# Fused attention and expert routing on one core: the first v kept on the chip, a new product order in the value step, and other places for loads and pads

## The chip, the core and the metric

The kernel runs on one core of one Trainium2 chip. The metric is the device time in microseconds of that core from the first to the last instruction of an execution, as the median of several runs. Five engines work side by side, each with its own stream of instructions in a fixed order: PE (TensorE, matrix products; PEld are its weight loads), DVE (VectorE), ACT (ScalarE), POOL (GpSimd) and SP (SyncE, which here issues most DMA transfers; its rows are named SPq).

## The reference, cut to what matters

```python
# u, v: (8, 2496, 256)   z: (8, 2496, 64)
scores = (z @ z^T) / S                      # per batch, S = 2496
attn   = maximum(scores, 0) ** 2
x      = u * (attn @ v)                     # 8 * 2496 = 19968 rows of 256
xn, en = x / (norm(x) + 1e-6), expert_emb / (norm(expert_emb) + 1e-6)
logits = xn @ en.T / tau                    # 8 experts
e      = argmax(logits);  gate = softmax(logits)[e]
out    = gate * (maximum(x @ w1[e], 0) @ w2[e])   # w1: 256 x 1024, w2: 1024 x 256
```

## The kernel before

Everything is computed with pairs of 16-bit numbers: a float32 operand is scaled by a power of two and split into a high and a low half, and a product becomes two or three products of halves. The scale comes from the largest absolute value, so z and v of a batch have to be scanned (`scan_load`, `scan_max`, `scale_pieces`) before they can be split (`z_split`, `v_split`).

**First part: attention and routing.** Each of the 8 batches has 20 key tiles `s` of 128 rows (the last has 64) and 5 query groups `g` of 512 columns (the last has 448): 800 steps. A step computes, where the score tile isn't had by symmetry, two products for the scores (`scores`), then ACT's Relu and Square make the probabilities, and DVE splits them into a high part (a cast) and a low part (a subtraction) in `parts`. `values` then adds to the two accumulators of the group: for each half `k` of the 256 output columns, high v times high part (`va`, `ph`), high v times low part (`va`, `pl`), low v times high part (`vb`, `ph`). A tile with `s // 4 > g` is also turned by a DMA transpose on SP into `tt`, for use in a later group. The split parts lie in five buffers (`hl`); scores run three tiles ahead (LOOK), parts two. When a group is finished, `route` makes a queue of some 20 small pieces, of which one is done per step of the next group: multiply by u, turn, norms, logits, choice of the expert, place, and at the end four indirect writes (`scatter`, POOL) of the group's rows into `xs` in DRAM, sorted by expert. In between the next batch is scanned, loaded and split (`ahead`), and the 8 experts' weights are scaled, split and written to DRAM (`weights`, 80 pieces, one in 8 steps, buffers wr1, wr2 and wo).

Ahead of all that stands the start: z of batch 0 is scanned and split, v is scanned in 8 pieces through 2 buffers, and then loaded a second time tile by tile for the split. The small constants for the routing (identity, triangle, normalised expert embeddings) are made in the same place.

**Second part: experts.** The sorted rows are worked off in slots: 61 slots of 256 rows (phase A, whose rows come from the first seven batches), 10 of 256 (C) and 17 of 128 (B), with 4 spare ones. `slot_x` loads a slot's rows from `xs` with a DMA transpose, `slot_w` loads the expert's weights into one of 4 buffers (after the first ones under a condition: only if the expert changed), `slot_up` and `slot_down` are the two layers. The rows of slot k + 3 are asked for in slot k. The last pieces of routing, the tables of the phases C and B and the `pads` (8 rows of zeros behind each expert's rows) are popped from the same queue between the products of the first slots. Rows and weights go through SP, one instruction after the other. POOL writes the results to the output by an indirect DMA.

PE's order is that of the code (`manual_schedule`), SP's too from `slot_first` on. The other engines, and SP before that, follow a scheduler.

Of the kernel before, what the change touches and what calls it, by code (L numbers as in the profile page):

```python
# [19 lines left out]
P = 128  # L20
# [24 lines left out]
def relu2_attention_then_moe(ctx, tc, zT, uT, v, emb, tau, w1, w2, ident, tri, iota_e, out):  # L45
    nc = tc.nc
    B, DQ, S = zT.shape
    D = uT.shape[1]
# [14 lines left out]
    twin = S % P == DQ  # L63
# [11 lines left out]
    xs = dram.tile([E * CAP + TB, ROW], F32, name="xs")  # L75
    wsd = dram.tile([E, P, WR1 + WR2], F16, name="wsd")
# [18 lines left out]
    SCAN = S * DQ // (P * ZSCANS)  # L95
    assert S * DQ == ZSCANS * SCAN * P and DQ % ZSCANS == 0 and S % VSCANS == 0
    scan = {}

    def scan_load(b, what, i):

        t = wk.tile([P, SCAN], F32, name="scan", tag="scan", bufs=2)
        if what == "z":
            src = zT[b, i * (DQ // ZSCANS):(i + 1) * (DQ // ZSCANS), :]
        else:
            src = v[b, i * (S // VSCANS):(i + 1) * (S // VSCANS), :]
        nc.sync.dma_start(t, src.rearrange("a c -> (a c)").rearrange("(p w) -> p w", p=P))
# [60 lines left out]
    def z_load(b, c0):  # L167
        zt = zpool.tile([P, ZC], F32, name="zt", tag="zt", bufs=3)
        c1 = min(c0 + ZC, SP)
        m = min(c1, S) - c0  # L170
        if c1 > S and not twin:
            nc.gpsimd.memset(zt, 0.0)
        for h in (0, DQ):
            if m > 0:
                nc.sync.dma_start(zt[h:h + DQ, :m], zT[b, :, c0:c0 + m])
            if c1 > S and twin:
                nc.sync.dma_start(zt[h:h + DQ, m:m + DQ], zT[b, :, S - DQ:])
# [17 lines left out]
    def v_load(b, s):  # L195
        n = min(P, S - s * P)
        vt = wk.tile([P, D], F32, name="vt", tag="vt", bufs=VAHEAD + 2)
        if n < P and not twin:
            nc.gpsimd.memset(vt, 0.0)
        nc.sync.dma_start(vt[:n], v[b, s * P:s * P + n, :])  # L200
        if n < P and twin:
            nc.sync.dma_start(vt[n:], v[b, s * P:s * P + n, :])
        vraw[b, s] = vt

    def v_split(b, s):
# [3 lines left out]
        if twin and s == NST - 1:  # L209
# [53 lines left out]
    def values(acc, b, g, s, ph, pl, ks=(0, 1)):  # L263
# [3 lines left out]
        for k in ks:  # L267
            va = vv[:, k * P:(k + 1) * P]
            vb = vv[:, D + k * P:D + (k + 1) * P]
            if twin and last:  # L270
                nc.tensor.matmul(acc[k][:, :n], va, ph[:, :n], start=first, stop=False)
                nc.tensor.matmul(acc[k][:, :n], vb, pl[:, :n], start=False, stop=True)
                continue
            nc.tensor.matmul(acc[k][:, :n], va, ph[:, :n], start=first, stop=False)  # L274
# [11 lines left out]
    def route(b, g, acc, ut):  # L286
# [131 lines left out]
        def scatter(j):  # L418
            def f():
                m = min(P, n - j * P)  # L420
                nc.gpsimd.indirect_dma_start(  # L421
                    xs[:, :], bass.IndirectOffsetOnAxis(ap=loc["dsti"][:m, j:j + 1], axis=0),
                    row[:m, j, :], None)
            return f
# [99 lines left out]
    nc.vector.memset(ones_f, 1.0)  # L524
    for what, i in SCANS[:ZSCANS]:
        scan_load(0, what, i)
    nc.sync.dma_start(idt, ident)
    z_tiles(0)
    ZN = ceil_div(SP, ZC)
    for k in range(min(3, ZN)):  # L530
        z_load(0, k * ZC)
    for what, i in SCANS[:ZSCANS]:
        scan_max(0, what, i)
    for f in scale_pieces(0, "z"):
        f()
    for k in range(min(2, ZN)):
        z_split(0, k * ZC)
    for what, i in SCANS[ZSCANS:]:
        scan_load(0, what, i)
        scan_max(0, what, i)  # L540
    for q in range(min(VAHEAD, NST)):
        v_load(0, q)
# [4 lines left out]
    for i in range(min(LOOK - 1, len(direct))):  # L547
        halves[direct[i]] = parts(*direct[i], probs.pop(direct[i]))
    zk = 2
# [530 lines left out]
```

## Time and profile before

| | us |
|---|---|
| median of 3 runs (lowest to highest) | 2231.42 (2230.69 to 2233.59) |
| the profiled execution's own time | 2233.2 |
| its span, first to last instruction | 2231.4 |
| PE busy | 2149.6 (96%) |
| PE weight loads busy | 1411.3 (63%) |
| DVE busy | 1412.9 (63%) |
| ACT busy | 1089.9 (49%) |
| POOL busy | 349.7 (16%) |

The page gives the busy time of each engine over the span and in 40 slices, with the clock granted to PE and the share of the 16 DMA engines. The ends of PE's products are modelled, so a busy PE isn't a PE at its peak; what counts there is how far apart two products start. Attention runs to about 1352 us, phase A begins there. A row of the order of time has the start, the duration, the engine, the line, the operation, what it writes and reads with the shapes, and in brackets how long the engine was idle before it and what released it.

### The profile page before, as it was taken

What the parts mean: (1) busy time and instruction counts of PE and PEld (TensorE: products, weight loads), DVE (VectorE), ACT (ScalarE), POOL (GpSimd) and SP (SyncE); (2) the same over time, 40 slices, a digit from 0 to 9 for tenths busy, and PEclk for the clock granted to TensorE, in tenths of its full rate; (3) what the DMA queues carried; (4) which work ended last, traced back from release to release, by engine and by line L of the source; (5) the groups of instructions that cost most, each with busy time, mean ns of one, the idle gap of its engine ahead of it and who ended that gap; (6) DMA issues with size and microseconds to landing.
All of it is one profiled execution on the core that took longest, in us unless ns stands there. A gap on an engine that the chain in (4) does not pass through costs nothing. (4 is left out here: it accounts for less than half of the span.)

```text
span 2231.4 us, 42157 instructions
## 1 busy us (share of the span) xinstructions
PE 2149.6 (96%) x14634; PEld 1411.3 (63%) x14634; DVE 1412.9 (63%) x4174; ACT 1089.9 (49%) x2193; POOL 349.7 (16%) x428
## 2 busy tenths in 40 slices
PE   5999999999999999999999998999999999999997
PEld 2445445445445444445445556888888888888986
DVE  7788889788789888889788754433333333333332
ACT  5667667667568567667667542222222222222211
POOL 0011111111111111111111111211111111111211
PEclk9999999999999999999999999999999999999999
DMA  7948866765947857766756435433323332257383
GB/s 196 208 110 216 172 172 144 185 155 140 229 103 180 203 114 196 167 175 144 171 122 126 97 82 154 130 70 89 87 56 87 95 87 49 56 143 202 103 211 91
DMA packets 525322, 307.74 MB, mean 138 GB/s; under 512 B 444069, under 2 KB 486446, under 8 KB 516912
## 3 DMA queue, kind: packets, MB, share of 16 engines
q1 hardware_dynamic: 509920, 263.76, 51.2%
q0 software_dynamic: 15184, 41.24, 5.4%
q8 instruction: 117, 1.92, 0.4%
q14 instruction: 101, 0.83, 0.1%
HBM read 279.49 MB, written 59.60 MB: 152 GB/s over the span
## 5 line engine op out<-in xcount | busy, mean ns | idle before, releaser
L237 ACT ACTIVATE a<-sc 128x512 f32<-128x512 f32 (+1 forms) x480 | 283.1, 590 | 181.7 <-PE sc L235 126.8
L238 ACT ACTIVATE a<-a 128x512 f32<-128x512 f32 (+1 forms) x480 | 300.0, 625 | 13.5
L276 PEld LDWEIGHTS <-vv 128*128 128x128 f16 x1520 | 149.0, 98 | 183.7 <-issue 15.6
L876 POOL DMA_INDIRECT out_dram<-ot,me x159 | 155.0, 975 | 669.7 <-DVE ot L875 365.3
L871 PE MATMUL po<-w,hl 128*128 128x256 f16 x928 | 253.0, 273 | 0.0
L870 PE MATMUL po<-w,hh 128*128 128x256 f16 x928 | 252.9, 273 | 0.0
L869 PE MATMUL po<-w,hh 128*128 128x256 f16 x928 | 252.9, 273 | 0.0
L275 PEld LDWEIGHTS <-vv 128*128 128x128 f16 x1520 | 148.9, 98 | 160.9 <-issue 5.0
L421 POOL DMA_INDIRECT xs<-row,dsti x160 | 175.3, 1096 | 480.5 <-DMA xs<-row,dsti 344.1
L274 PEld LDWEIGHTS <-vv 128*128 128x128 f16 x1520 | 148.9, 98 | 157.9 <-issue 1.3
L274 PE MATMUL acc<-tt,vv 128*128 128x512 f16 (+1 forms) x640 | 236.4, 369 | 0.0
L275 PE MATMUL acc<-tt,vv 128*128 128x512 f16 (+1 forms) x640 | 236.3, 369 | 0.0
L276 PE MATMUL acc<-tt,vv 128*128 128x512 f16 (+1 forms) x640 | 236.2, 369 | 0.0
L875 DVE TENSOR_SCALAR ot<-po,me,w 128x256 f32<-128x256 f32 x116 | 58.3, 540 | 219.8 <-PE po L871 218.5
L234 PE MATMUL sc<-z 128*128 128x512 f16 (+1 forms) x480 | 182.4, 380 | 4.6 <-DVE z L191 4.6
L235 PE MATMUL sc<-z,z 128*128 128x512 f16 (+1 forms) x480 | 182.5, 380 | 0.0
L870 PEld LDWEIGHTS <-hh 128*128 128x128 f16 x1272 | 124.8, 98 | 20.4 <-issue 5.8
L871 PEld LDWEIGHTS <-hl 128*128 128x128 f16 x1272 | 124.8, 98 | 14.8
L869 PEld LDWEIGHTS <-hh 128*128 128x128 f16 x1272 | 124.8, 98 | 14.5
L323 ACT COPY x<-pt 128x264 f32<-128x264 f32 x160 | 59.6, 372 | 95.7 <-PE pt L313 85.6
L869 PE MATMUL po<-wb,hh 128*128 128x256 f16 x344 | 94.7, 275 | 5.5 <-DMA wb<-wsd 5.5
L870 PE MATMUL po<-wb,hh 128*128 128x256 f16 x344 | 94.8, 275 | 0.0
(4179 smaller groups left out, 5146.3 us busy)
## 6 DMA issues: line engine op xcount, KB each, us to landing
w<-wsd SPq DMA_DIRECT2D x64, 1026.0 KB
wa<-wsd SPq DMA_DIRECT2D x46, 1024.0 KB
w<-wsd SPq DMA_DIRECT2D x42, 1024.0 KB
wb<-wsd SPq DMA_DIRECT2D x24, 1026.0 KB
scan<-in_v_dram SPq DMA_DIRECT2D x64, 312.0 KB
vt<-in_v_dram SPq DMA_DIRECT2D x152, 128.0 KB
ut<-in_uT_dram SPq DMA_DIRECT2D x32, 512.0 KB
wr<-in_w_dram SPq DMA_DIRECT2D x16, 1024.0 KB
```

The lines of the kernel that those rows point to most:

```text
L234: nc.tensor.matmul(sc[:, :n], z1[:, ss], z1[:, t0:t0 + n], start=True, stop=False)
L235: nc.tensor.matmul(sc[:, :n], z1[:, ss], z2[:, t0:t0 + n], start=False, stop=True)
L237: state["at"] = nc.scalar.activation(a[:, :n], sc[:, :n], AF.Relu, scale=2.0 ** -SHIFT).ins
L238: nc.scalar.activation(a[:, :n], a[:, :n], AF.Square)
L274: nc.tensor.matmul(acc[k][:, :n], va, ph[:, :n], start=first, stop=False)
L275: nc.tensor.matmul(acc[k][:, :n], va, pl[:, :n], start=False, stop=False)
L276: nc.tensor.matmul(acc[k][:, :n], vb, ph[:, :n], start=False, stop=last)
L421: nc.gpsimd.indirect_dma_start(xs[:, :], bass.IndirectOffsetOnAxis(ap=loc["dsti"][:m, j:j + 1], axis=0), row[:m, j, :], None)
L869: nc.tensor.matmul(o, hh[:, f, t], wh, start=(f == 0), stop=False)
L870: nc.tensor.matmul(o, hh[:, f, t], wl, start=False, stop=False)
L871: nc.tensor.matmul(o, hl[:, f, t], wh, start=False, stop=(f == NF - 1))
L876: nc.gpsimd.indirect_dma_start(out, bass.IndirectOffsetOnAxis(ap=me.bitcast(U32)[:, j, 1:2], axis=0), ot[:, j, :], None, bounds_check=N - ...
```

## The change

1. z is put into DRAM twice on top of itself (128 rows), and z and v are padded with copies of their last 64 rows, so that a z chunk and a v tile are one load each. Scans are 640 columns wide instead of 624.
2. v of batch 0 is loaded once, in five pieces of four tiles, into buffers that later hold expert weights (`v_first`). The scan reads these pieces (1,024 columns each), and so does the split.
3. At the start four score tiles are computed ahead of v's scale instead of three; ACT and DVE follow the written order there. One z scan and the identity are issued from ACT. The routing constants are made at steps 6 and 14 of group 0, and the experts' weights begin at step 26 instead of 20.
4. `values` does all products with the high part first, for both halves, and then those with the low part.
5. The x loads of phase A name the last scatter of batch 6 as what they wait for, and none of batch 7's.
6. The second-layer load for the second buffer moves behind the x load of slot 3, `pads` 12 places down the queue (two slots), a slot's expert number and flag are read once, and the writes to the output don't wait for each other.

```diff
     def scan_max(b, what, i):
         if i == 0:
-            scan[b, what] = sml.tile([P, ZSCANS if what == "z" else VSCANS], F32, name="smx" + what)
+            n = ZSCANS if what == "z" else VSCANS if b else NV0
+            scan[b, what] = sml.tile([P, n], F32, name="smx" + what)
...
     def z_load(b, c0):
...
-        for h in (0, DQ):
-            if m > 0:
-                nc.sync.dma_start(zt[h:h + DQ, :m], zT[b, :, c0:c0 + m])
...
+        nc.sync.dma_start(zt[:, :c1 - c0], zT[b, :, c0:c1])
...
+    def v_first(i):
+        if not v0:
+            v0.extend([wp.tile([P, W1], F32, name="v0a", tag="wr1"), wp.tile([P, W2], F32, name="v0b", tag="wr2"),
+                       wp.tile([P, 2 * max(W1, W2)], F16, name="v0c", tag="wo").bitcast(F32)])
...
+        nc.sync.dma_start(t, v[0, q * P:(q + n) * P, :].rearrange("(j p) d -> p j d", p=P))
+        for j in range(n):
+            vraw[0, q + j] = t[:, j, :]
+        scan[0, "v", i] = t.rearrange("p j d -> p (j d)")
...
     def values(acc, b, g, s, ph, pl, ks=(0, 1)):
...
-            nc.tensor.matmul(acc[k][:, :n], va, ph[:, :n], start=first, stop=False)
-            nc.tensor.matmul(acc[k][:, :n], va, pl[:, :n], start=False, stop=False)
-            nc.tensor.matmul(acc[k][:, :n], vb, ph[:, :n], start=False, stop=last)
+        for va, vb, o in halves_:
+            nc.tensor.matmul(o, va, ph[:, :n], start=first, stop=False)
+            if not last:
+                nc.tensor.matmul(o, vb, ph[:, :n], start=False, stop=False)
+        for va, vb, o in halves_:
+            nc.tensor.matmul(o, vb if last else va, pl[:, :n], start=False, stop=last)
...
+    for i in range(NV0):
+        v_first(i)
...
-    for i in range(min(LOOK, len(direct))):
+    for i in range(LOOK + 1):
         probs[direct[i]] = scores(*direct[i])
...
-    wnext = NST
+    wnext = NST + 6
...
     def slot_x(k):
...
+        if SEQ[k][0] == "A":
+            need = mybir.DependencyInfo(mybir.DependencyClass.Sync, mybir.DependencyReason.DATA)
+            for d in got:
+                for other in puts.get(B - 1, []):
+                    tc.declare_no_dep(d.ins, other, reason="the first phase has rows of the batches routed by then")
+                tc.add_manual_dep(d.ins, puts[B - 2][-1].name, need, reason="rows of the batches routed by then")
...
     def slot_w(k, i):
...
-        e = nc.sync.value_load(tab[0:1, 1, c:c + 1], min_val=0, max_val=E - 1)
+        if ("e", k) not in mst:
+            mst["e", k] = nc.sync.value_load(tab[0:1, 1, c:c + 1], min_val=0, max_val=E - 1)
+            if k in after.values():
+                mst["new", k] = nc.sync.value_load(tab[0:1, 2, c:c + 1], min_val=0, max_val=1)
...
     def slot_down(k):
...
+            for other in mst["put"]:
+                tc.declare_no_dep(put, other, reason="each token has one row of out")
...
+        if i == 6:
...
+            nc.scalar.activation(esq, emb_sb, AF.Square, accum_out=en2)
+            enorm, _ = sqrt_of(en2, (E, 1), "e")
...
-    queue += ([table_c] if KC else []) + [table_b, pads]
+    queue += ([table_c] if KC else []) + [table_b] + [lambda: None] * 12 + [pads]
...
     slot_pools()
-    slot_w(opens[1], 1)
...
         if k + XAHEAD < KT:
             slot_x(k + XAHEAD)
+        if k == 0:
+            slot_w(opens[1], 1)
```

The order of instructions shows three places. On DVE, at the end of v's scan (smxv takes the maxima of the pieces, smv and sm1v the maximum of all, scv is the scale, en the embeddings, z1 and z2 the split z), before:

```order
L112 TENSOR_REDUCE smxv_144<-scan_164 128x1
L613 RECIPROCAL ede_283<-ede_283 8x1
L124 TENSOR_REDUCE smv_209<-smxv_144 128x1
L615 TENSOR_SCALAR en_286<-emb_sb_248,ede_283 8x256
L190 SCALAR_TENSOR_TENSOR z2_106<-zt_303,scz_132,z1_105 64x256
L128 TENSOR_REDUCE sm1v_213<-pm_211 1x1
L191 SCALAR_TENSOR_TENSOR z1_105<-zt_303,scz_132,z2_106 64x256
```

and after:

```order
L114 TENSOR_REDUCE smxv_173<-v0a_113 128x1 x2
L114 TENSOR_REDUCE smxv_173<-v0b_114 128x1 x2
L254 CAST hl__178<-a_152 128x512
L185 SCALAR_TENSOR_TENSOR z2_108<-zt_121,scz_139,z1_107 64x256
L255 TENSOR_TENSOR hl__178<-a_152,hl__178 128x512
L114 TENSOR_REDUCE smxv_173<-v0c_115 128x1
L186 SCALAR_TENSOR_TENSOR z1_107<-zt_121,scz_139,z2_108 64x256
L126 TENSOR_REDUCE smv_184<-smxv_173 128x1
L185 SCALAR_TENSOR_TENSOR z2_108<-zt_182,scz_139,z1_107 64x256
L186 SCALAR_TENSOR_TENSOR z1_107<-zt_182,scz_139,z2_108 64x256
L130 TENSOR_REDUCE sm1v_188<-pm_186 1x1
```

Five reductions stand close together, the embeddings are gone from here, and only one probability tile is split by then (three before).

On PE, the first value step before (hl is the probability tile with both parts, vv the split v):

```order
L274 MATMUL acc0_316<-hl__193,vv_320 128x512
L275 LDWEIGHTS vv_320
L275 MATMUL acc0_316<-hl__193,vv_320 128x512
L276 LDWEIGHTS vv_320
L276 MATMUL acc0_316<-hl__193,vv_320 128x512
L274 LDWEIGHTS vv_320
L274 MATMUL acc1_317<-hl__193,vv_320 128x512
L275 LDWEIGHTS vv_320
L275 MATMUL acc1_317<-hl__193,vv_320 128x512
L276 LDWEIGHTS vv_320
L276 MATMUL acc1_317<-hl__193,vv_320 128x512
```

and after:

```order
L279 MATMUL acc0_248<-hl__178,vv_252 128x512
L281 LDWEIGHTS vv_252
L281 MATMUL acc0_248<-hl__178,vv_252 128x512
L279 LDWEIGHTS vv_252
L279 MATMUL acc1_249<-hl__178,vv_252 128x512
L281 LDWEIGHTS vv_252
L281 MATMUL acc1_249<-hl__178,vv_252 128x512
L283 LDWEIGHTS vv_252
L283 MATMUL acc0_248<-hl__178,vv_252 128x512
L283 LDWEIGHTS vv_252
L283 MATMUL acc1_249<-hl__178,vv_252 128x512
```

L275 before and L283 after read the low part: it moved from the second place to the fifth, with as many products and weight loads as before.

On SP, from the x load of slot 3 to the conditional weight load of slot 1, before (xt16 and me are a slot's rows, wa0 the weights, Atab the table of phase A):

```order
L813 DMA_TRANSPOSE xt16_16985<-xs_72 128x4x256
L815 ISA
L815 DMA me_16987<-xs_72 128x2x4
L821 TENSOR_LOAD Atab_15523
L821 ISA x2
L826 TENSOR_LOAD Atab_15523
L826 ISA x2
L827 ISA
L827 DMA wa0_16752<-wsd_73 128x4096
```

and after, behind the last transpose of the attention:

```order
L262 DMA_TRANSPOSE tt_16371<-hl__16436 128x8x64
L810 ISA
L810 DMA w11_16802<-wsd_73 128x4104
L804 TENSOR_LOAD Atab_15371
L804 ISA x2
L806 TENSOR_LOAD Atab_15371
L806 ISA x2
L812 ISA
L812 DMA wa0_16600<-wsd_73 128x4096
```

The x load is gone from there. It stands, with those of slots 0 to 2 and the first weights, far ahead, among the transposes of batch 7's group 1, which begin with tt_15499:

```order
L789 DMA_TRANSPOSE xt16_16612<-xs_72 128x4x256
L791 ISA
L791 DMA me_16614<-xs_72 128x2x4
L804 TENSOR_LOAD Atab_15371
L804 ISA x2
L810 ISA
L810 DMA wa0_16600<-wsd_73 128x4096
L810 ISA
L810 DMA wb0_16602<-wsd_73 128x4104
L262 DMA_TRANSPOSE tt_15499<-hl__15496 128x8x128
```

Before, the first of these transposes followed the load of u with nothing but the read of a table in between.

## Rows read from the trace of the kernel before

**Rows 1.** Stretches: from:to us, length, busy per engine (xcount), PEclk, DMA share, GB/s

```profile
0.00:30.00 30.00, 5.03 (x15) 2.33 (x16) 21.36 (x70) 11.21 (x22) 1.08 (x10) 1.00 0.72 214
30.00:71.00 41.00, 37.40 (x159) 15.92 (x159) 32.01 (x71) 34.36 (x69) 0.00 (x0) 1.00 0.86 190
1350.00:1431.00 81.00, 65.42 (x545) 55.37 (x543) 36.14 (x146) 17.79 (x37) 15.62 (x17) 0.89 0.42 127
2140.00:2176.00 36.00, 31.16 (x397) 29.23 (x395) 11.02 (x17) 6.97 (x12) 4.92 (x6) 0.95 1.03 242
2176.00:2217.00 41.00, 40.75 (x538) 38.23 (x535) 14.25 (x23) 8.36 (x14) 8.71 (x9) 1.00 0.44 119
```

**Rows 2.** PE's waits over the span: who <- for whom: us in total, times, longest

```profile
PE pm L126 <- DVE smv L124: 12.0, 2, 11.5
PE ph__17115 L845 <- DMA wa<-wsd: 9.9, 1, 9.9
...
PE po L869 <- DMA wb<-wsd: 5.5, 2, 4.7
...
PE ph__30232 L845 <- DMA wa<-wsd: 4.0, 1, 4.0
```

**Rows 3.** Order of time, DVE at the start, and PE's first product of group 1

```profile
9.16 0.80 DVE L112 TENSOR_REDUCE smxv<-scan 128x1 f32<-128x624 f32 x1 [1.07 <-DMA scan<-in_v_dram]
...
11.40 0.48 DVE L191 SCALAR_TENSOR_TENSOR z<-zt,scz,z 64x256 f16<-64x256 f32 x1
...
14.38 0.42 DVE L244 CAST hl__193<-a 128x512 f16<-128x512 f32 x1
14.83 0.69 DVE L245 TENSOR_TENSOR hl__193<-a,hl__193 128x512 f16<-128x512 f32 x1
...
25.97 0.16 DVE L124 TENSOR_REDUCE smv<-smxv 128x1 f32<-128x8 f32 x1
...
29.57 0.15 DVE L140 TENSOR_SCALAR scv<-spwv 128x1 int32<-128x1 int32 x1
...
70.82 0.38 PE L274 MATMUL acc<-tt,vv 128*128 128x512 f16 x1
```

**Rows 4.** Order of time, PE, two products in a row on different accumulators

```profile
34.59 0.38 PE L276 MATMUL acc<-hl__196,vv 128*128 128x512 f16 x1
34.81 0.38 PE L274 MATMUL acc<-hl__196,vv 128*128 128x512 f16 x1
```

**Rows 5.** PE's waits for a low part, 75 to 1350 us, first and last

```profile
PE acc L275 <- DVE hl__12436 L245: 0.8, 1, 0.8
...
PE acc L275 <- DVE hl__5324 L245: 0.2, 1, 0.2
```

**Rows 6.** Order of time, SP, the x load of slot 1

```profile
1343.14 3.92 SPq L813 DMA_TRANSPOSE xt<-xs  x1
```

**Rows 7.** Order of time, POOL and SP, the border of the phases

```profile
1364.12 0.96 POOL L421 DMA_INDIRECT xs<-row,dsti  x1 [1.75 <-DMA xs<-row,dsti]
1366.73 1.25 SPq L813 DMA_TRANSPOSE xt<-xs  x1
...
1415.95 8.24 SPq L792 DMA_DIRECT2D xs<-pad  x8
```

**Rows 8.** Stretches behind two long waits of PE, columns as in rows 1

```profile
607.30:610.60 3.30, 3.20 (x10) 1.54 (x11) 2.35 (x5) 0.89 (x3) 0.00 (x0) 0.55 1.01 319
1365.40:1375.60 10.20, 5.31 (x25) 4.04 (x26) 0.69 (x1) 1.49 (x4) 0.00 (x0) 0.50 0.41 82
```

**Rows 9.** Order of time, SP, first-layer loads of two slots of 128 rows

```profile
2147.65 0.34 SPq L827 DMA_DIRECT2D wa<-wsd  x1
...
2154.21 0.34 SPq L827 DMA_DIRECT2D wa<-wsd  x1
```

**Rows 10.** Order of time, DVE and POOL, the last result and its write

```profile
2216.79 0.54 DVE L875 TENSOR_SCALAR ot<-po,me,w 128x256 f32<-128x256 f32 x1 [2.08 <-PE po L871]
...
2219.15 0.97 POOL L876 DMA_INDIRECT out_dram<-ot,me  x1 [3.19 <-issue]
```

More of the change, by code (lines that the diff above doesn't have):

```diff
@@ L62, in relu2_attention_then_moe @@
     S2 = float(S) * float(S)
-    twin = S % P == DQ
+    assert S % P == DQ and zT.shape[2] == v.shape[1] == SP
     GT = 512 // P
@@ L94, in relu2_attention_then_moe, with scan_load @@
     ZSCANS, VSCANS = 2, 2 * D // DQ
[L95 to L96 removed]
+    SCAN = SP * DQ // (P * ZSCANS)
+    assert SP * DQ == ZSCANS * SCAN * P and DQ % ZSCANS == 0 and SP % VSCANS == 0
     scan = {}
[L99 removed]
+    def scan_load(b, what, i, eng=None):
         t = wk.tile([P, SCAN], F32, name="scan", tag="scan", bufs=2)
@@ L208, in v_split @@
         k = scan[b, "cv"]
-        if twin and s == NST - 1:
+        if s == NST - 1:
             lo, hi = slice(0, DQ), slice(DQ, P)
@@ L266, in values @@
         first, last = s == 0, s == NST - 1
[L267 to L270, printed above, removed]
-                nc.tensor.matmul(acc[k][:, :n], va, ph[:, :n], start=first, stop=False)
-                nc.tensor.matmul(acc[k][:, :n], vb, pl[:, :n], start=False, stop=True)
-                continue
-            nc.tensor.matmul(acc[k][:, :n], va, ph[:, :n], start=first, stop=False)
-            nc.tensor.matmul(acc[k][:, :n], va, pl[:, :n], start=False, stop=False)
-            nc.tensor.matmul(acc[k][:, :n], vb, ph[:, :n], start=False, stop=last)
+        halves_ = [(vv[:, k * P:(k + 1) * P], vv[:, D + k * P:D + (k + 1) * P], acc[k][:, :n]) for k in ks]
+        for va, vb, o in halves_:
[4 more added lines that the diff above has]
+            nc.tensor.matmul(o, vb if last else va, pl[:, :n], start=False, stop=last)
     def u_load(b, g):
@@ L524, in relu2_attention_then_moe @@
     nc.vector.memset(ones_f, 1.0)
+    first = tc.manual_schedule(engines={mybir.EngineType.DVE, mybir.EngineType.Activation})
+    first.__enter__()
     for what, i in SCANS[:ZSCANS]:
-        scan_load(0, what, i)
-    nc.sync.dma_start(idt, ident)
+        scan_load(0, what, i, nc.scalar if i % 2 else nc.sync)
+    nc.scalar.dma_start(idt, ident)
     z_tiles(0)
     ZN = ceil_div(SP, ZC)
-    for k in range(min(3, ZN)):
+    for k in range(2):
         z_load(0, k * ZC)
+    for i in range(NV0):
+        v_first(i)
+    z_load(0, 2 * ZC)
     for what, i in SCANS[:ZSCANS]:
@@ L794, in relu2_attention_then_moe @@
     nc.sync.dma_start(xs[E * CAP:E * CAP + TB, :], pad[:TB])
-    mst = {"ph": 0}
+    mst = {"ph": 0, "put": []}
     queue = []
@@ L939, in relu2_attention_then_moe @@
             zk += 1
-        if own and nd + LOOK < len(direct):
+        if own and nd + LOOK < len(direct) and direct[nd + LOOK] not in probs:
             st = direct[nd + LOOK]
@@ L1037, in layout @@
     N = B * S
+    pad = -S % P
+    zp = np.concatenate([z, z[:, S - pad:]], axis=1)
     p = np.arange(P, dtype=np.float32)[:, None]
```

157 lines of the change are left out of this document (80 added, 77 removed).

## The prediction

> **What bounds the kernel now.** I read the table of stretches first. TensorE (PE) is busy almost everywhere, so the time is PE's own work plus the stretches in which it waits or runs at its lower clock. Four stretches show such time [rows 1]: the first 30 us (5.03 busy), 30 to 71 (37.40 of 41), 1350 to 1431 (65.42 of 81, mean granted clock 0.89) and 2140 to 2176 (31.16 of 36, 0.95). The list of PE's waits names what ends them [rows 2]: the scan of v (12.0 us), one load of first-layer weights at the border to the expert phase (9.9), two of second-layer weights (5.5, of them 4.7 at the border), one load late in the run (4.0). Then I followed each wait in the order of time to what was really late. PE's order is written by hand, and the change keeps it but for the start and the order inside one value step, so PE's work stays, and each term below is a wait that goes, shrinks or appears. The sum is made against the profiled span, 2231.4 us; the median of the runs is 2231.42, so nothing is added.
>
> **Start: 4 us gained (0 to 6).** Before, v's scale is known at 29.57 + 0.15 = 29.72 us [rows 3]: the eight pieces of v, from the reduction at 9.16 on, go through two buffers. After, five pieces of 1,024 columns are loaded without such a limit. Bytes ahead of the last landing: 0.66 MB of z scan, 0.07 of identity, 0.26 of z, 2.62 of v, 3.6 MB in all. The first 30 us moved 214 GB/s at a DMA share of 0.72 [rows 1], so 297 at a full share: 12 us, and about 3 to the first landing, so 15. At a mere 214 GB/s it is 20. VectorE is the later one: its first z splits ended at 11.40 + 0.48 = 11.88, with a reduction of 0.80 and a wait of 1.07 for it in between, so now at 10.0 to 11.1; I take 10.3. A reduction of 1,024 columns costs 0.80 x 1024/624, at most 1.3, and with a fixed part like the 0.16 of the small one about 1.22; five of them, a cast 0.42, a low part 0.69, two z halves and the last reduction make 8.3, with gaps 8.6 [rows 3]. That is 18.9, against 25.97 + 0.16 before. The chain from there to the scale took 29.72 - 26.13 = 3.6 us and has the same links, so 22.5: 7.2 us earlier.
>
> Not all of it reaches the end of group 0, which PE leaves at 70.82 [rows 3]. VectorE was busy 32.0 us in 30 to 71 [rows 1], and more is now left for it at that point: counted in its new order, two more probability tiles (2 x 1.11), one z piece (0.95), the expert normalisation that stood ahead of the scale and now lies among steps 6 to 14 (some 20 small operations, about 4.2), and about one v split and some small steps (1.2): 8.6 more, 40.6 us, with gaps 42.7. From 22.5 on that is 65.2, and PE's last products put the end of group 0 near 66, 4.8 us earlier. If VectorE idles as it did before (9 us of 41) nothing is left. I take 4, near the count, since v now lies on the chip and VectorE waits for no v load. The two loads issued from ACT cost ACT under 1 us while it has nothing to do. v's tiles lie in buffers of expert 0's weights, whose load now waits for the v splits; it is due at step 26, and its 80 pieces, one in 8 steps, end at step 660 of 800, so nothing waits.
>
> **High-part products first: 4 us gained (0 to 6).** In a value step PE needed the low part of the probabilities for its second product, now for its fifth. Three products of 512 columns lie between, 0.22 us each [rows 4], 0.65 in all. Between 75 and 1350 us the list has nine waits for a low part, 0.8 to 0.2 us, 4.5 in all [rows 5]. Each shrinks by up to 0.65, which leaves under 1; shorter ones, which the list leaves out, go too; but PE comes earlier to the next tile, and some of it comes back there. Waits for a high part and for routing aren't touched.
>
> **First-phase loads moved to batch 7: 1.5 us lost (0 to 4).** The order shows the x tiles of slots 0 to 3 and three weight loads of 1 MB among the transposes of batch 7's group 1. They wait for batch 6's last scatter, and the transposes behind them on SP wait with them. Before, these loads stood at the end, and an x load behind them took 3.92 us to issue [rows 6] instead of 1.25 [rows 7], so a queue behind 3 MB fills. The probability transposes now stand behind 2 to 3 MB, land some 7 to 10 us late, and hold VectorE's five buffers. PE's lead is two steps, 3.5 us. A stall of 1 to 3 us remains, once.
>
> **Border, first wait: 11.7 us gained (9 to 12.4).** SP is one queue. The x load of slot 3 waited there for the last scatter of group (7,3), issued at 1364.12; it went at 1366.73, and the conditional weight load of slot 1 behind it [rows 7]. PE had waited 9.9 for that [rows 2], and in the 10.2 us around its restart the granted clock was 0.50, the 1.2 GHz level, with 5.31 us of work in it [rows 8]; half of that, 2.7, is the price. After, the four x loads are long done and the conditional load waits for PE alone. I leave 0.9, as SP must still see PE finish slot 0, and routing pieces now come in a tighter row: 9.9 + 2.7 - 0.9.
>
> **Border, pads two slots later: 7 us gained (0 to 7).** The eight pad rows waited on SP until 1415.95 for the last scatters, and then took 8.24 us of its time [rows 7], with the weights of slot 4 behind them: PE's 4.7 [rows 2]. A mean clock of 0.89 over 81 us [rows 1] means 17.8 us at the lower level; 10.2 belong to the first wait, and of the other 7 some 4 are work, so 2 more. After, the pads stand two slots later. A slot has 96 products of half the columns above, 0.11 us, so 10.5 us. By then the scatters have landed, and what is queued behind the pads (weights of slot 7, x of slot 9) is needed two slots on. So the 8.24 us are hidden; without that cover the 7 stay.
>
> **Late loads: 5.5 us gained (2 to 6.8).** In the 128-row slots SP needs 2154.21 - 2147.65 = 6.56 us a slot [rows 9]. PE needs less: a slot has 72 products, and 538 took 40.75 us [rows 1], so 5.45. SP falls behind until PE waits 4.0 and then 0.8 (the rest of the 5.5), and the clock, 0.95 over 36 us, costs 1.8. After, expert and flag are read once a slot instead of twice; the second load then stands without its two reads, about 1.5 us, so SP needs 5.0, less than PE. What may stay is a load whose transfer alone is late.
>
> **End: 1.7 us gained (0 to 1.7).** The last scatter to the output waited for the one before it: 2219.15, while its tile was ready at 2217.33 [rows 10]. After, only the tile counts.
>
> **One z load instead of two, scans of 640 columns:** nothing either way. SP and VectorE have room beside PE there; uncovered, the scans cost 10 x 0.02 us a batch.
>
> Sum: 4 + 4 - 1.5 + 11.7 + 7 + 5.5 + 1.7 = 32.4, so 2231.4 - 32.4 = **2199 us**. With all lower ends 7 is gained, 2224; with all upper ends 40, 2191.
>
> **Rivals.** *The early part gives back.* VectorE idles in group 0 as before (0), the low-part waits come back at the next tile (1), and the hoisted loads stall PE for 4 us, with 1.7 for the clock: 0 + 1 - 5.7 + 11.7 + 7 + 5.5 + 1.7 = 21, 2210 us. For it: VectorE is the one to wait for up to 71 us. Against it: in the count above its operations find their inputs there.
>
> *All at the upper end:* 2191.
>
> *The first phase still waits.* If the x loads, or what stands ahead of slot 1's weights, still hold for group (7,3)'s scatters, 11.7 stays: 2211. Against it: in the order they stand ahead of that group's transposes.
>
> *Slower.* The new value step changes the accumulator four times instead of twice. If PE paused at these changes, its clock would fall. One fall, at 607 us, shows 0.55 over 3.3 us [rows 8], so 3 us at the lower level, about 1.6 lost with PE busy. From 20 falls on the gain is gone; one in each of the 40 groups costs 64, so 2263 us. Against it: at a change of accumulator two products start 0.22 us apart [rows 4], as much as inside one. The Trainium skill speaks for it (TensorE: Matmul & The Clock Gate, section A second HAM failure mode: psum-queue depth-cycling): in a kernel with 512 columns that cycled through PSUM banks, PE paused a little between groups, and the clock went down and up again. By that rule the time would be the slower one just given; the row speaks against it, and I go by the row.
>
> **How the numbers follow.** Forecast 0.60 (2192 to 2207), early part gives back 0.20, all at the upper end 0.10, first phase still waits 0.06, slower 0.04. The range leaves out the slower case, the far half of the lower ends and what lies past the upper ones: 2188 to 2214. A measurement of this kernel tells 0.2%, 4.5 us, from no change; all cases but the last lie beyond that, and 0.02 goes to sums that I overlooked: faster 0.94, same 0.02, slower 0.04.
>
> **What the profile will show.** Right: v's scale near 22.5 us; group 0 left near 66; no wait over 1.5 us at slots 0 to 2 and none behind the pads; under 1 us of waits in the 128-row slots; no new wait over 3 us at the transposes of batch 7's group 1. Wrong: v's scale after 26; products more than 0.22 us apart in the value steps, or a lower mean clock in 71 to 1350; the conditional load of slot 1 later than 2 us after slot 0's last product.

## The result, and the profile after

The changed kernel takes 2205.64 us (median of 4 runs, 2203.21 to 2208.33) beside 2232.51 (2230.69 to 2234.13) for the kernel before: a ratio of 0.988, 95% interval 0.9863 to 0.9897. The profiled span went from 2231.4 to 2204.6 us, 26.8 less; the forecast was 32.4 less (2199, range 2188 to 2214). Direction and range held. Of the terms of the sum, two came out lower than forecast (by 7 us and by up to 4) and one higher (by 4).

The stretches of the changed kernel that answer to [rows 1], with the same columns (from:to us, length, busy per engine, PEclk, DMA share, GB/s):

```profile
0.00:23.00 23.00, 5.48 (x14) 2.27 (x14) 15.33 (x40) 11.17 (x21) 1.08 (x10) 1.00 0.83 259
23.00:62.30 39.30, 37.46 (x159) 16.11 (x160) 33.91 (x97) 33.95 (x70) 0.00 (x0) 1.00 0.87 185
1236.00:1267.00 31.00, 25.20 (x114) 11.02 (x113) 18.03 (x55) 14.49 (x27) 3.16 (x5) 0.97 0.92 209
1340.00:1420.00 80.00, 78.86 (x681) 65.97 (x680) 43.85 (x177) 21.41 (x44) 17.90 (x20) 1.00 0.41 126
2110.00:2150.00 40.00, 38.47 (x518) 36.08 (x516) 13.87 (x23) 8.96 (x15) 6.82 (x7) 1.00 1.04 282
```

The start is shorter by 7 us; the border (fourth line) is full, with PE busy 78.86 of 80 us at a granted clock of 1.00, where before it was 65.42 of 81 at 0.89. The third line is new: near 1236 us, in batch 7, PE is busy only 25.20 of 31 us, in a place where the kernel before lost nothing. PE's longest waits over the whole span, as in [rows 2] (who <- for whom: us in total, times, longest):

```profile
PE pt L317 <- DVE xt L311: 4.5, 3, 3.3
PE pm L128 <- DVE smv L126: 4.2, 1, 4.2
...
PE acc L279 <- DVE hl__15652 L254: 1.4, 1, 1.4
...
PE ph__28676 L830 <- DMA wa<-wsd: 1.2, 1, 1.2
```

The wait for v's scale fell from 11.5 to 4.2, the waits of 9.9 and 4.7 for weights are gone, and that of 4.0 fell to 1.2. The 3.3 for the evicted sums (L311) is the new stretch in batch 7.

To place the whole difference I took, from the start times of all matmuls, the distance from each to the next, less the median distance for its line and shape, and summed that excess by stretch. The medians alone sum to 2122.8 to 2122.9 us in every kernel here, so the rest is what PE loses, whether it waits or runs at the lower clock. "First" is the start of the first matmul, "end" the time from the last matmul's start to the end of the span.

| us lost by PE | first + 0–75 | 75–1235 | 1235–1285 | 1285–1450 | 1450 on | end | span |
|---|---|---|---|---|---|---|---|
| before | 34.5 | 30.5 | 0.0 | 21.0 | 7.8 | 14.9 | 2231.4 |
| changed | 26.8 | 28.3 | 8.9 | 1.8 | 2.8 | 13.4 | 2204.6 |
| gained | 7.7 | 2.2 | −8.9 | 19.2 | 5.0 | 1.5 | 26.8 |
| forecast | 4 | 4 | −1.5 | 18.7 | 5.5 | 1.7 | 32.4 |

### The profile page after: what moved, and what is told of

The parts are those of the page before. It is cut to its first block, busy times and chain, and to the rows that moved or that the text cites. A ratio compares the mean times of both kernels' runs of the same rounds, so it can differ in the third digit from the quotient of the medians.

```text
span 2204.6 us, 41435 instructions
## 1 busy us (share of the span) xinstructions
PE 2146.6 (97%) x14634; PEld 1408.8 (64%) x14634; DVE 1406.0 (64%) x4171; ACT 1087.7 (49%) x2193; POOL 348.3 (16%) x428
## 5 line engine op out<-in xcount | busy, mean ns | idle before, releaser
L283 PEld LDWEIGHTS <-vv 128*128 128x128 f16 x1600 | 157.2, 98 | 186.0 <-issue 8.8
L279 PEld LDWEIGHTS <-vv 128*128 128x128 f16 x1600 | 156.9, 98 | 168.4 <-issue 2.4
L281 PEld LDWEIGHTS <-vv 128*128 128x128 f16 x1520 | 149.2, 98 | 168.5 <-issue 12.9
L279 PE MATMUL acc<-tt,vv 128*128 128x512 f16 (+1 forms) x640 | 236.4, 369 | 0.0
L281 PE MATMUL acc<-tt,vv 128*128 128x512 f16 (+1 forms) x640 | 236.2, 369 | 0.0
L283 PE MATMUL acc<-tt,vv 128*128 128x512 f16 (+1 forms) x640 | 184.0, 369 | 0.0
L854 PE MATMUL po<-wb,hh 128*128 128x256 f16 x344 | 93.8, 273 | 0.4 <-DMA wb<-wsd 0.4
L856 PE MATMUL po<-wb,hl 128*128 128x256 f16 x344 | 93.8, 273 | 0.0
```

Source lines behind the costliest of these rows:

```text
L279: nc.tensor.matmul(o, va, ph[:, :n], start=first, stop=False)
L281: nc.tensor.matmul(o, vb, ph[:, :n], start=False, stop=False)
L283: nc.tensor.matmul(o, vb if last else va, pl[:, :n], start=False, stop=last)
L854: nc.tensor.matmul(o, hh[:, f, t], wh, start=(f == 0), stop=False)
L856: nc.tensor.matmul(o, hl[:, f, t], wh, start=False, stop=(f == NF - 1))
```

## Experiments

Each is the changed kernel with one edit (e8 has two, e11 none). Medians are of 4 or 5 runs (e6 is a single run); ratios are to the kernel before, whose median was 2229.5 to 2233.1 us beside them. The theory formed from the table: the missing gain lies in batch 7, where the hoisted first-phase loads stand among the tile transposes. The main rival: the new order of the products is worth less than nothing.

**What happens in batch 7.** SP's transfers of the changed kernel in order of time (start, us, engine, line, operation, out<-in). The `tt` transposes are the twelve of batch 7's group 1; `wa`, `wb` are expert weights of 1 MB, `xt`, `me` rows of the first slots:

```profile
1229.79 1.42 SPq L789 DMA_TRANSPOSE xt<-xs  x1
1231.42 0.42 SPq L791 DMA_DIRECT2D me<-xs  x1
1232.67 0.36 SPq L810 DMA_DIRECT2D wa<-wsd  x1
1233.22 0.35 SPq L810 DMA_DIRECT2D wb<-wsd  x1
1233.68 3.31 SPq L262 DMA_TRANSPOSE tt<-hl__15496  x1
1237.84 0.36 SPq L810 DMA_DIRECT2D wa<-wsd  x1
1238.30 2.76 SPq L262 DMA_TRANSPOSE tt<-hl__15515  x1
1241.15 3.70 SPq L262 DMA_TRANSPOSE tt<-hl__15557  x1
...
1251.11 1.24 SPq L262 DMA_TRANSPOSE tt<-hl__15632  x1
...
1258.36 1.25 SPq L262 DMA_TRANSPOSE tt<-hl__15695  x1
```

What VectorE (DVE) waits for there (who <- for whom: us in total, times, longest):

```profile
DVE hl__15799 L254 <- DMA tt<-hl__15695: 3.5, 1, 3.5
DVE hl__15743 L254 <- DMA tt<-hl__15632: 2.6, 1, 2.6
DVE hl__15652 L254 <- DMA tt<-hl__15515: 1.9, 1, 1.9
DVE hl__15632 L254 <- DMA tt<-hl__15496: 1.7, 1, 1.7
DVE hl__15672 L254 <- DMA tt<-hl__15557: 1.1, 1, 1.1
```

And the casts that end two of these waits, in order of time:

```profile
1246.19 0.43 DVE L254 CAST hl__15652<-a 128x512 f16<-128x512 f32 x1 [1.94 <-DMA tt<-hl__15515]
...
1254.35 0.43 DVE L254 CAST hl__15743<-a 128x512 f16<-128x512 f32 x1 [2.58 <-DMA tt<-hl__15632]
```

A probability tile has five buffers, and the cast into one waits until the transpose that reads the tile five earlier has landed. The transpose of 15515 was issued at 1238.30 and released its buffer at 1246.19, 7.9 us later; that of 15632, behind no weights, at 1251.11 and 1254.35, 3.2 us. While the weights were on the queue a transpose also held SP for 2.76 to 3.70 us instead of 1.24. So the first three waits are late landings, and the last two are late issues: by then SP was some 8 us behind (the tile of 15632 was ready at 1243.35), and rows stood between. PE waits 1.4, 0.4, 0.4 and 0.2 for tiles and at last 3.3 for the sums of group 1, whose eviction stands behind the 3.5 us wait on VectorE. Right behind that wait of 3.3 the trace shows the granted clock at 0.50 for 3.4 us from 1265.3 on; with PE busy, that is up to 1.7 of the 8.9.

**The loads behind the transposes.**

```diff
-            nc.sync.dma_start_transpose(turned[b, g, h][:, :, c:c + m], hl[:m].rearrange("p a t -> p (a t)"))
+            state["tt"] = nc.sync.dma_start_transpose(turned[b, g, h][:, :, c:c + m], hl[:m].rearrange("p a t -> p (a t)")).ins
...
-            slot_first()
+            with tc.issue_after(state["tt"]): slot_first()
```

> The changed kernel with the first seven loads of the expert phase (x rows of slots 0 to 3 and three weight blocks) put behind batch 7's last tile transpose on SP; each engine's own order stays. Theory: the 8.9 us that TensorE loses between 1235 and 1285 us come from these loads (3 MB of weights slow the landing of the transposes from 3.1 to 7.8 us, and SP issues loads among them, so that VectorE waits for free tiles); they go, and nothing new comes at 1350 us: 2205.6 - 8.9 = 2196.7 us, 2195 to 2199. Rival: the loss there comes from the new order of the products or from batch 7's routing; then it stays, and the time is 2205 to 2207. Second rival: the loads are now too late for slot 0 and the wait comes back at 1350 us, 2205 or above.

Measured: 2195.99 us (2193.88 to 2196.16), ratio 0.9832 [0.9819, 0.9845]. The stretch 1235 to 1285 lost 0.0 again and 1285 to 1450 lost 1.8 as in the changed kernel. Theory right: moving seven loads, with each compute engine's own order the same, gives back the 8.9 us.

**Weights or rows?** Three kernels divide the seven loads (slot 3's rows are late in all three). In e9 and e10 `state["tt"]` is set as in e2, to the last transpose. In e12 `state["tt", b]` lists the transposes of a batch; 20 and 23 are the fifth and the eighth of group 1.

In e9 rows early, weights late:

```diff
-        slot_x(0)
-        slot_w(0, 0)
-        slot_w(0, 1)
-        slot_w(opens[1], 0)
-        for k in range(1, XAHEAD):
+        for k in range(XAHEAD):
             slot_x(k)
+        with tc.issue_after(state["tt"]):
+            slot_w(0, 0)
+            slot_w(0, 1)
+            slot_w(opens[1], 0)
```

In e10 weights early, rows late:

```diff
-        slot_x(0)
         slot_w(0, 0)
         slot_w(0, 1)
         slot_w(opens[1], 0)
-        for k in range(1, XAHEAD):
-            slot_x(k)
+        with tc.issue_after(state["tt"]):
+            for k in range(XAHEAD):
+                slot_x(k)
```

In e12 rows in their places among the transposes, weights late:

```diff
         slot_x(0)
-        slot_w(0, 0)
-        slot_w(0, 1)
-        slot_w(opens[1], 0)
-        for k in range(1, XAHEAD):
-            slot_x(k)
+        for k, q in ((1, 20), (2, 23)):
+            with tc.issue_after(state["tt", B - 1][q]): slot_x(k)
+        with tc.issue_after(state["tt", B - 1][-1]):
+            slot_w(0, 0); slot_w(0, 1); slot_w(opens[1], 0)
```

> The changed kernel with the first three weight loads (3 MB) and slot 3's rows put behind batch 7's last tile transpose, while the x loads of slots 0 to 2 stay ahead of batch 7's first transposes on SP. If the transfer of the weights is what holds the transposes up, the loss between 1235 and 1285 us falls from 8.9 to below 3 us (2197 to 2200); if it is SP's time for the x loads (3.4 us each, 10 us for three), it stays above 4 us (2201 to 2206).

> The changed kernel with the x loads of slots 0 to 3 put behind batch 7's last tile transpose, while the first three weight loads (3 MB) stay ahead of its first transposes on SP: the other half of the kernel with late weights and early rows, which lost nothing between 1235 and 1285 us. If the transfer of the weights alone holds the transposes up, the loss there stays near 8.9 us (6 to 9; 2203 to 2206 us in all). If it takes both, the weights' transfer and the x loads among the transposes, it falls to between 0 and 4 us (2196 to 2200).

> The changed kernel with the first three weight loads and slot 3's rows put behind batch 7's last tile transpose, while the rows of slots 0 to 2 keep the places on SP that they have in the changed kernel: slot 0's ahead of the twelve transposes of batch 7's group 1, slot 1's and 2's among them. If the 3 MB of weights, started when these transposes begin, are what costs the 8.9 us between 1235 and 1285 us, the loss is below 1 us (2194 to 2198); if SP's time for the rows among the transposes costs part of it, the loss is 2 to 5 us (2198 to 2201).

Measured: e9 2194.43 us (2191.53 to 2195.14), 0.9831 [0.9815, 0.9847]; e10 2194.16 (2192.06 to 2195.87), 0.9828 [0.9814, 0.9841]; e12 2194.77 (2191.52 to 2196.27), 0.9832 [0.9814, 0.985]. In 1235 to 1285 they lost 0.0, 0.0 and 1.0. e10 was meant to show what the weights alone cost, and doesn't: without slot 0's rows ahead of them, which wait for batch 6's last scatter, the weights went out 11 to 15 us earlier and were out of the way. SP in e10:

```profile
1220.36 0.37 SPq L810 DMA_DIRECT2D wa<-wsd  x1
...
1222.03 0.35 SPq L810 DMA_DIRECT2D wb<-wsd  x1
1223.18 0.35 SPq L810 DMA_DIRECT2D wa<-wsd  x1
1230.78 1.29 SPq L262 DMA_TRANSPOSE tt<-hl__15496  x1
```

e12 does tell: the rows of slots 1 and 2 keep their places, the weights are gone from among the transposes, and one DVE wait of the five is left, with PE nearly full and its longest wait at 0.4 us (the same stretch as the third line of the first table of stretches, then DVE's wait):

```profile
1236.00:1267.00 31.00, 30.45 (x153) 14.88 (x151) 18.52 (x63) 16.11 (x35) 4.77 (x6) 1.00 0.65 131
```
```profile
DVE hl__15799 L254 <- DMA tt<-hl__15695: 2.9, 1, 2.9
```

So rows of two slots among the transposes cost 1.0 us by themselves. The other 7.9 need the 3 MB of weights on the queue in the very microseconds in which the transposes begin; some 10 us earlier (e10) or 80 us later (e2, e9, e12) the same weights cost nothing. Rows ahead of the transposes cost nothing either (e9), though SP issued the first of them there 5.0 us after its tile was ready (1229.22 and 1234.25). What the weights would cost at that moment with no rows behind them was not run.

**The order of the products.**

```diff
         for va, vb, o in halves_:
             nc.tensor.matmul(o, va, ph[:, :n], start=first, stop=False)
+            nc.tensor.matmul(o, vb if last else va, pl[:, :n], start=False, stop=last)
             if not last:
-                nc.tensor.matmul(o, vb, ph[:, :n], start=False, stop=False)
-        for va, vb, o in halves_:
-            nc.tensor.matmul(o, vb if last else va, pl[:, :n], start=False, stop=last)
+                nc.tensor.matmul(o, vb, ph[:, :n], start=False, stop=last)
```

e1 is this edit alone, e8 this edit with the late loads of e2.

> The changed kernel with one part undone: the low-part product stands between the two high-part products of each half again. The prediction's step says that the new order is worth about 4 us, so 2205.6 + 4 = 2209.6 us, and TensorE's waits between 75 and 1350 us grow from 37 to about 41 us, with low-part waits back. Theory after reading the trace: VectorE delivers the high part of a tile as late as the low part, so that outside the stretch 1235 to 1285 us the order only moves the wait from the second product to the first (28 us lost there in the changed kernel, 30 in the one before); then 2203.6 to 2207.6 us.

> Two parts of the changed kernel otherwise: the first seven loads of the expert phase stand behind batch 7's last tile transpose, and the low-part product stands between the two high-part products again. If the order of the products is worth nothing, the time is that of the kernel with only the late loads, 2196.0 us, within 2194 to 2198; if it is worth the 4 us of the prediction, 2200; if the old order is better by the 3 us that the kernel with the old order alone was faster, 2193.

Measured: e1 2202.54 us (2201.21 to 2204.32), 0.9866 [0.9851, 0.9881], 3 us below the changed kernel; e8 2196.63 (2193.53 to 2199.63), 0.9841 [0.9825, 0.9857], 0.6 us above e2. In the time the old order costs nothing that can be seen. In 75 to 1235 us the two old-order kernels lost 25.4 and 30.0 us.

**The changed kernel once more**, for the scatter of that stretch.

> The changed kernel itself, once more, beside the others on one chip: to see how far its time and TensorE's loss between 75 and 1235 us move with nothing changed. By the five kernels with the same order of engines in that stretch (24.3 to 30.6 us lost there) the time should lie within 2202 to 2208 us and the loss within 24 to 31 us; the loss between 1235 and 1285 us should be 8.4 to 9.4 us again. If the loss there falls under 5 us instead, it hangs on chance and not on the place of the loads.

Measured: 2205.59 us (2203.08 to 2213.06), 0.9878 [0.9862, 0.9895]. The loss in batch 7 was 8.5 us again, but 75 to 1235 lost 35.7, past what I expected (the profile is of the slowest of the four runs). Eleven profiles with the new order (the changed kernel twice, e2 to e7, e9, e10, e12) lie between 24.3 and 35.7, mean 27.8; the two with the old order have a mean of 27.7. An effect of 2 us there can't be told.

Most of this scatter is the clock. Between 75 and 1235 us the traces show PE at the lower level, a granted clock of 0.50, for 10.2 us in all in the changed kernel, 20.5 in e11, 0 in e1, 10.2 in e8 and 3.4 to 10.2 in the other nine, and the loss follows this time (correlation 0.94 over the 13 profiles). The 10.3 us more of e11 come, at half pace, to about 5 of its 7.4. Every such fall comes during a wait of PE or close behind one, but the same wait does not always bring a fall: at 520.2 us in the changed kernel a wait of 3.7 ends and the clock is down from 521.2 to 524.6, at 516.7 in e1 one of 3.4 ends and the clock stays up. Less half of the time at the lower level, the new order loses 22 to 26 us, 23.6 on average, and the old one 25.4 and 24.9: a hint of 1.5 us for the new order, on two profiles, and no more.

**Rows wait for all batches.**

```diff
-        if SEQ[k][0] == "A":
-            need = mybir.DependencyInfo(mybir.DependencyClass.Sync, mybir.DependencyReason.DATA)
-            for d in got:
-                for other in puts.get(B - 1, []):
-                    tc.declare_no_dep(d.ins, other, reason="the first phase has rows of the batches routed by then")
-                tc.add_manual_dep(d.ins, puts[B - 2][-1].name, need, reason="rows of the batches routed by then")
```

> The changed kernel with one part undone: the first phase's x loads wait for every batch's scatters again, as before. The prediction's two steps: the first wait of the border comes back (+11.7) and the cost of the early loads (1.5) goes: 2205.6 + 10.2 = 2215.8 us. Theory after reading the trace: the border's +11.7 comes back, but 8.9 us at 1235 to 1285 us go: 2205.6 + 2.8 = 2208.4 us, 2207 to 2210.

Measured: 2203.48 us (2202.2 to 2203.81), 0.9866 [0.9851, 0.9882]: 2.2 below the changed kernel, not 2.8 above. By stretch the theory holds: 1235 to 1285 lost 0.0, and 1285 to 1450 lost 12.0, 10.2 more than the changed kernel. PE's wait at the border is back:

```profile
PE ph__16936 L830 <- DMA wa<-wsd: 7.9, 1, 7.9
```

That is 1.3 us more in these two places; what made the time shorter is 75 to 1235, 24.3 us here (3.4 at the lower clock) and 28.3 and 35.7 (10.2 and 20.5) in the two profiles of the changed kernel, that is, the scatter just told. As the change placed them, the early loads cost about what they gain.

**Pads at once.**

```diff
-    queue += ([table_c] if KC else []) + [table_b] + [lambda: None] * 12 + [pads]
+    queue += ([table_c] if KC else []) + [table_b] + [pads]
```

> The changed kernel with one part undone: the pads go out right behind the tables again, two slots earlier. The prediction's step: TensorE's wait of 4.7 us near 1421 us comes back and half clock for some us behind it, 2205.6 + 7 = 2212.6 us, 2210 to 2213. Rival: with the first phase's x loads waiting for seven batches only, the pads stand in nobody's way, and the time stays at 2205.6.

Measured: 2207.62 us (2205.41 to 2209.42), 0.989 [0.9874, 0.9906]. 1285 to 1450 lost 7.8, 6.0 more than the changed kernel; PE's wait there, and SP's pads:

```profile
PE po L854 <- DMA wb<-wsd: 4.2, 1, 4.2
```
```profile
1399.78 8.80 SPq L768 DMA_DIRECT2D xs<-pad  x8
```

The rival (pads stand in nobody's way) is out by this wait and this stretch; the time rose by 2.0 only, below the 2210 that I expected, and could not have told.

**Expert and flag read twice.**

```diff
-        if ("e", k) not in mst:
-            mst["e", k] = nc.sync.value_load(tab[0:1, 1, c:c + 1], min_val=0, max_val=E - 1)
-            if k in after.values():
-                mst["new", k] = nc.sync.value_load(tab[0:1, 2, c:c + 1], min_val=0, max_val=1)
+        mst["e", k] = nc.sync.value_load(tab[0:1, 1, c:c + 1], min_val=0, max_val=E - 1)
+        if k in after.values():
+            mst["new", k] = nc.sync.value_load(tab[0:1, 2, c:c + 1], min_val=0, max_val=1)
```

> The changed kernel with one part undone: a slot's expert number and its flag are read from the table for each of its two weight loads again. The prediction's step: SP falls behind TensorE in the 128-row slots again and 5.5 us of waits come back after 2100 us: 2205.6 + 5.5 = 2211.1 us. Theory after reading the trace (the changed kernel lost 2.8 us after 1450 us, the one before 7.8): 2205.6 + 5.0 = 2210.6 us. Rival: SP has time enough in the large slots to be ahead, and the late loads come early for another reason: 2205 to 2207.

Measured: 2208.96 us (2206.09 to 2213.36), 0.99 [0.9884, 0.9916]. From 1450 us on PE lost 6.9, 4.1 more than the changed kernel; the longest wait, for first-layer weights, is 3.9 for 1.2. SP's first-layer loads of two slots in e5, and then in the changed kernel:

```profile
2129.59 0.34 SPq L812 DMA_DIRECT2D wa<-wsd  x1
...
2135.66 0.34 SPq L812 DMA_DIRECT2D wa<-wsd  x1
```
```profile
2124.48 0.34 SPq L812 DMA_DIRECT2D wa<-wsd  x1
...
2129.46 0.34 SPq L812 DMA_DIRECT2D wa<-wsd  x1
```

For these two slots it is 6.07 us a slot against 4.98: with PE's 5.45 in between, SP falls behind in the one and not in the other. The two extra reads of a slot thus took 1.1 us of SP's time.

**Output scatters chained.**

```diff
-            for other in mst["put"]:
-                tc.declare_no_dep(put, other, reason="each token has one row of out")
-            mst["put"].append(put)
```

> The changed kernel with one part undone: the scatters of the output wait for one another again. The prediction's step: the end behind the last product grows by 1.7 us, from the 13.4 us of the changed kernel to about 15.1. Rival: the last scatter waits for VectorE anyway, and the end stays at 13.4. Only the end is read; the whole time can't tell 1.7 us.

Measured, in a single run: the end is 15.1 us, against 13.4. POOL's last scatter in e6 and in the changed kernel:

```profile
2190.78 0.97 POOL L861 DMA_INDIRECT out_dram<-ot,me  x1 [3.31 <-issue]
```
```profile
2192.35 0.97 POOL L861 DMA_INDIRECT out_dram<-ot,me  x1 [1.64 <-DVE ot L860]
```

It comes 2.79 us after the last matmul's start (2187.99) with the chain and 1.13 (2191.22) without.

**v scanned, then loaded.**

```diff
-    for i in range(NV0):
-        v_first(i)
...
-    for i in range(NV0):
+    for i in range(VSCANS):
+        scan_load(0, "v", i)
         scan_max(0, "v", i)
-        if i == NV0 - 2:
+        if i == VSCANS - 1:
+            for q in range(VAHEAD):
+                v_load(0, q)
+        if i == VSCANS - 2:
...
             v_split(b, s)
+            if s + VAHEAD < NST:
+                v_load(b, s + VAHEAD)
```

> The changed kernel with one part undone: the first batch's v is scanned for its scale in eight pieces and then loaded a second time, instead of being kept on chip; the other changes of the start stay. The prediction's step: v's scale comes 7 us later, near 29.7 us, but group 0 is bound by VectorE's work and is left only 4 us later, at 66: 2205.6 + 4 = 2209.6 us. Theory after reading the trace: group 0 takes 39.4 us from the scale (22.9 to 62.3 us) and not 42.7, nothing in it waits for VectorE for long, so that what the scale loses the end loses: 2205.6 + 7 = 2212.6 us, 2211 to 2215.

Measured: 2212.19 us (2209.32 to 2212.33), 0.9902 [0.9887, 0.9917], 6.6 above the changed kernel. The scale's last step and PE's first product of group 1, in e7 and in the changed kernel:

```profile
30.16 0.15 DVE L142 TENSOR_SCALAR scv<-spwv 128x1 int32<-128x1 int32 x1
...
69.19 0.38 PE L279 MATMUL acc<-tt,vv 128*128 128x512 f16 x1
```
```profile
22.72 0.15 DVE L142 TENSOR_SCALAR scv<-spwv 128x1 int32<-128x1 int32 x1
...
62.26 0.38 PE L279 MATMUL acc<-tt,vv 128*128 128x512 f16 x1
```

From the scale to the end of group 0 it takes 38.9 and 39.4 us. The scale is 7.4 us earlier than in e7 and the end of group 0 6.9: nearly all that the scale gains, the end of group 0 gains.

## Why the prediction was right, and where it was wrong

**Start: forecast 4, measured 7.7.** The scale came at 22.72 + 0.15 = 22.87 us for a forecast 22.5. The step that failed is the one that let VectorE set the end of group 0; its count of VectorE's work, 40.6 us, of them 8.6 added to the 32.0 of [rows 1], was too long. In 23.0 to 62.3 us VectorE was busy 33.91, so 1.9 was added, and PE 37.46 of 39.30: PE sets the pace there, group 0 was left at 62.26 and not near 66, and the gain of the scale was not used up. Part of PE's pace there is the clock: up to 29.65 us its products start 0.43 us apart (last section). Keeping v on chip is 5.5 us of the 7.7 (e7, up to 75 us); the rest belongs to the other edits of the start, which were not parted.

**High-part products first: forecast 4, not found in the time.** The first half of the step held: waits for probability tiles did shrink. PE's waits for them in 75 to 1235 us (those that the list has, over 0.15 us) sum to 3.5 to 5.8 us in the eleven profiles of the new order, 4.8 on average, to 7.9 in e1 and 7.7 in e8 with the old one, and to 6.3 in the kernel before. The step that failed is the size of "some of it comes back there": PE's other waits of the stretch, for routing and for evicted sums, are 10.0 to 12.8 us, 11.1 on average, in the new order, against 9.2 and 8.8 in e1 and e8 and 10.9 before. All waits together are 15.9 on average beside 17.1 and 16.4, and 17.2 before: about 1 us is left of the 4, less than the scatter. That the other waits grew through the order is not shown. Two late tiles in e8 (old order: low part at L280, high part at L279) and in the changed kernel (low part at L283):

```profile
PE acc L280 <- DVE hl__5512 L255: 1.0, 1, 1.0
...
PE acc L279 <- DVE hl__5512 L254: 0.8, 1, 0.8
...
PE acc L280 <- DVE hl__11431 L255: 0.8, 1, 0.8
...
PE acc L279 <- DVE hl__11431 L254: 0.4, 1, 0.4
```
```profile
PE acc L279 <- DVE hl__5512 L254: 1.7, 1, 1.7
...
PE acc L279 <- DVE hl__11431 L254: 0.4, 1, 0.4
...
PE acc L283 <- DVE hl__5512 L255: 0.4, 1, 0.4
```

At 11431 the wait fell from 1.2 us to 0.4. At 5512, the latest tile, it only moved from the low part to the high part: 1.8 and 2.1 us.

**First-phase loads in batch 7: forecast −1.5, measured −8.9.** Place and mechanism were foretold (transposes behind 2 to 3 MB, five buffers held), and the size was not. The failed step is "a stall of 1 to 3 us remains, once": transposes landed some 8 us late, as forecast (15515 was ready at 1234.81 and landed by 1246.19, where 3.2 us are usual), but SP also lost time in issuing them, so the lateness went on through all twelve, PE waited five times, 5.7 us in all, and the last wait hit the eviction of the whole group. The sign that the prediction had named, no new wait over 3 us there, failed with 3.3. This alone is 7.4 us, more than the 5.6 by which the sum was too high. That the start's surplus of 3.7 paid for part of it is luck; without it the time would have been near 2209, still within the range.

**Border: forecast 11.7 + 7, measured 19.2.** Right, with the mechanism: at slots 0 to 2 no wait is over 0.5 us, the granted clock in 1340 to 1420 is 1.00, and the pads' eight rows, 8.26 us on SP from 1410.31 on, keep nobody waiting. Undone one at a time the two parts cost 10.2 (e3) and 6.0 (e4); the 3.0 that are missing from 19.2 show only with both undone, as before. There the same two waits were 9.9 and 4.7 us, and singly they are 7.9 and 4.2, which is 2.5 of the 3.0; why they are shorter singly was not traced.

**Late loads: forecast 5.5, measured 5.0 (4.1 by e5).** Right: SP needs 4.98 us a slot for the forecast 5.0. The sign "under 1 us of waits in the 128-row slots" was missed: waits of 1.2 and 0.4 are left there. **End: forecast 1.7, measured 1.5 (1.7 by e6).** Right.

**The rivals.** "The early part gives back" had the right loss (5.7 for the loads) with a wrong companion (VectorE idle in group 0), and gave 2210; the result lies between it and the forecast. "The first phase still waits" is out by the border. "Slower" is out: the changed kernel starts two products on different accumulators as far apart as two on the same one. One of the signs set for it did appear: over 71 to 1350 us the mean granted clock is 0.99 (1.00 before). It is not the order's doing: e2, with the new order and late loads, has 1.00, as have e1 and e8 with the old one, and one of the four falls behind the 0.99 is that of batch 7. Three products of a value step, of which the third changes the accumulator:

```profile
1258.00 0.38 PE L279 MATMUL acc<-tt,vv 128*128 128x512 f16 x1
1258.21 0.38 PE L281 MATMUL acc<-tt,vv 128*128 128x512 f16 x1
1258.43 0.38 PE L279 MATMUL acc<-tt,vv 128*128 128x512 f16 x1
```

The Trainium skill's rule that was weighed there (TensorE: Matmul & The Clock Gate, section A second HAM failure mode: psum-queue depth-cycling) describes short pauses between groups of products in a kernel that cycled through PSUM banks, and a clock that went down and up by them; at 0.21 and 0.22 us a product this trace has no such pause with two accumulators in turn.

## What to carry to other kernels

When a dependency is loosened, look where the freed transfers land in their queue. Here the loads moved up by more than 100 us, and 3 MB in front of small transposes that free a ring of five buffers, with rows among them, cost 8 to 9 us, while the same loads some 10 us earlier or 80 us later cost none. Behind a scale or another late start, check which engine really sets the pace before subtracting for it. A reordering that shortens many waits for one slow producer should be priced by all waits of the stretch together, and against how far that stretch moves by itself: here up to 3 us of such waits went, about 1 of all, beside a scatter of 11.

With the loads out of the way the kernel beats both: 2194 to 2196 us (e2, e9, e10, e12), 0.983 of the kernel before.

## What the runs showed of the hardware

A transposing DMA on SP's queue held SP for 1.24 us, and for 2.76 to 3.70 us when loads of 1 MB stood ahead of it; its landing went from 3.2 to 7.9 us after its issue.

The column of the granted clock can read 1.00 where the trace has no record of the clock yet. In the changed kernel products of 512 columns started 0.43 us apart from 24.71 to 29.0 us, against 0.21 to 0.22 from 29.75 on:

```profile
24.71 0.63 PE L279 MATMUL acc<-hl__178,vv 128*128 128x512 f16 x1
25.14 0.63 PE L281 MATMUL acc<-hl__178,vv 128*128 128x512 f16 x1
```

Its trace has no clock record before 29.65 us. That of e11, the same kernel, begins at 15.8 and shows the lower level, 1.2 GHz, from 19.2 to 29.5. The same stretch in the changed kernel and in e11, with the columns of [rows 1]:

```profile
19.30:29.40 10.10, 6.65 (x16) 2.47 (x17) 7.96 (x28) 6.20 (x14) 0.00 (x0) 1.00 0.61 184
```
```profile
19.30:29.40 10.10, 6.63 (x16) 2.47 (x17) 7.96 (x28) 6.32 (x15) 0.00 (x0) 0.50 0.59 183
```

The record of the kernel before begins at 34.16 us, so the 1.00 in the first line of [rows 1] tells nothing either.

One program moves by itself: the changed kernel lost 28.3 us in 75 to 1235 us in one profile and 35.7 in another, with the order of every engine the same, and with 10.2 and 20.5 us of that stretch at the lower clock.
